# One-token attention over a 65,536-row cache with a gated FFN on one core: V partly past four columns of p, q in rows, wo in one bank, and looped programs

## The chip, the core and the metric

The kernel runs on one core of a Trainium2 chip. The metric is the device time of one execution in microseconds. Three runs of the kernel before gave 2518.55, 2518.58 and 2518.63 us (median 2518.58). The times inside the kernel come from one more execution, taken by the hardware profiler. Engines are called as the profile calls them: PE (matmul), PEld (its weight loads), DVE (vector), ACT (scalar), POOL, SP (which only issues transfers here).

## The reference, cut to what matters

```python
# B = Sq = 1, D = 512, H = 32 heads, Sk = 65536, Dh = 128, F = 1792, all bf16
q = (x @ wq).reshape(H, Dh)
scores = einsum("hd,hkd->hk", q, k_cache) * Dh ** -0.5
p = softmax(scores)
o = einsum("hk,hkd->hd", p, v_cache)
a = o.reshape(H * Dh) @ wo
b = (silu(x @ w_gate) * (x @ w_up)) @ w_down
g = sigmoid((x * gate_w).sum())
out = g * a + (1 - g) * b
```

K and V are 537 MB each and every byte of them is used once; the weights are about 14 MB.

## The kernel before

**Tiling.** A head's K and V come in two halves each ("first place" and "second place", u = 0 and 1). A half is 128 partitions of 256 rows of 128 numbers, 64 KB per partition and 8 MB in all, fetched by one transfer. The four places lie in one buffer `ring` of 176 KB per partition and overlap: K's second place begins in the middle of the first (32 KB against 0), V's first place at 96 KB and its second at 112 KB, `wq` at 144 KB for the start. So a transfer may be issued only when the part of the ring that it overwrites has been read.

**Order of the transfers.** SP issues them in one written-out list (L132-178): for head r, K's first place once half of the K second place before it is turned (`ktd`), V's second place of head r-1 once PE has passed rows 64 to 255 of V's first place (`va1`), K's second place once half of K's first is turned, V's first place once PE has finished the last head's V (`vbd`). Head 31 adds `wo`; then come the FFN weights, and the last head's V second place in six parts (`PARTS`, L114), whose last five wait for `va1`, so that PE can follow them as they land; the last two 128 KB slices of `w_down` end the list.

**Scores.** For each chunk of 16 rows DVE transposes 32-bit pairs into `kt` (`turn`, L274-278, four buffers), and PE runs four matmuls with `kt` moving, 512 columns each, against a sparse copy of q (`zq`), into `psS` (`scores`, L346-351). After both places DVE takes the maximum, POOL spreads it over the partitions, ACT takes the exponential into `pa`, DVE transposes it to `pb` (L300-302, L226-231).

**Values.** `values` (L353-358) runs one matmul per row of V: the 128x128 block of V is the stationary operand (it is loaded by a LDWEIGHTS), one column of `pb` moves past it, and the result gathers in one column of `psO`:

```python
last = nc.tensor.matmul(psO[:, 0:1], at(base + r * 256, Dh), pb[:, col:col + 1], ...)
```

**Order on PE.** A small loop of named bodies (L374-432): `pe_ka` (scores of K's first place), `pe_vb` (V's second place of the head before, waiting for the six marks `s_vb`, `s_p2` to `s_p6`, which for all heads but the last were counted up beforehand), `pe_kb` (scores of K's second place, then V's first place: rows 64 to 255, then 0 to 63). Before `pe_kb` of head 31 comes `pe_wo` (heads 0 to 30 times `wo`), after it `pe_mlp` (gate and up, 112 matmuls at L412, the wait for `guT`, then 12 slices of `w_down`), then `pe_vb` once more for head 31's V second place, and `pe_end` with the last slices and head 31's share of `wo`. Products with a row of `wo` or `w_down` go through `rows` (L360-364), as two matmuls of 256 columns, one into `psY` row 0 and one into `psZ` row 64.

**Other places that the change touches.** q is made by 128 matmuls with `wq` stationary and x moving (L335-339). SP, ACT and POOL have all 32 heads written out; DVE runs a loop over the heads; PE runs the bodies above.

Of the kernel before, what the change touches and what calls it, by code (L numbers as in the profile page):

```python
# [5 lines left out]
P = 128  # L6
KB = 1024
CH = 16
# [4 lines left out]
V_CUT = 64  # L13
# [13 lines left out]
def bass_gated_mix__mha_block_cached__swiglu_ffn__decode_kernel(  # L27
# [27 lines left out]
    with ExitStack() as ctx:  # L55
# [6 lines left out]
        def sem(name):  # L62
# [8 lines left out]
        psZ = psum("psZ", [P, 512], F32)  # L71

# [17 lines left out]
        fin = sb("fin", [P, D], BF16)  # L90
        sc = sb("sc", [P, 8], F32)
        xTb = sb("xTb", [P, 16], BF16)
# [5 lines left out]

        names = ("s_x s_wq s_k0a s_k0b s_ka s_kb s_va s_vb s_wo s_wo1 s_wg s_wu s_wd s_wd2 s_wd3 s_p2 s_p3 s_p4 s_p5 s_p6 "
                 "s_ones s_qd s_ramp s_rampT s_id s_sel s_z s_zb s_e1 s_g s_xT s_xTb s_q s_qTb s_qs s_zq s_h s_sig s_gu s_dch s_ach "  # L100
                 "ktd qkd va1 vbd s_mx s_ar s_nb s_exp s_pb s_L s_li s_otn s_o s_om s_wod s_o31 s_y0 s_y1 s_fin s_out")
# [12 lines left out]
        PARTS = ((192, 256), (0, 118), (118, 164), (164, 182), (182, 189), (189, 192))  # L114
# [17 lines left out]
        @block.sync  # L132
        def _(sp):
            def load(dst, src, s):
                sp.dma_start(dst, src).then_inc(sm[s], 16)  # L135

            def place(kind, h, u, s):
                byte = {"k": (K_A, K_B), "v": (V_A, V_B)}[kind][u]
                load(at(byte, ROWS * Dh), kv_dram[kind][h, u], s)

            k0 = kv_dram["k"][0, 0]
            k1 = kv_dram["k"][0, 1]
            half = ROWS * Dh // 2
            load(at(K_A + 2 * half, half), k0[:, half:2 * half], "s_ka")
            load(at(K_A, half), k0[:, 0:half], "s_k0a")
            load(at(K_B + 2 * half, half), k1[:, half:2 * half], "s_k0b")
            sp.wait_ge(sm["ktd"], NCH // 2)
            load(at(K_B, half), k1[:, 0:half], "s_kb")
            sp.wait_ge(sm["s_q"], 1)
            place("v", 0, 0, "s_va")  # L150
            for r in range(1, H):
                sp.wait_ge(sm["ktd"], PER * r - NCH // 2)
                place("k", r, 0, "s_ka")
                sp.wait_ge(sm["va1"], r)
                place("v", r - 1, 1, "s_vb")
                if r == L:
                    wo_dram = A_wo.rearrange("(p j) n -> p (j n)", j=32)
                    for q in range(2):
                        sp.wait_ge(sm["ktd"], PER * r + 3 * NCH // 4 + q * NCH // 4)
                        load(at(WO + q * 16 * KB, 16 * D), wo_dram[:, q * 16 * D:(q + 1) * 16 * D], "s_wo")  # L160
                sp.wait_ge(sm["ktd"], PER * r + NCH // 2)
                place("k", r, 1, "s_kb")
                sp.wait_ge(sm["vbd"], r + 1)
                place("v", r, 0, "s_va")
            sp.wait_ge(sm["s_wod"], 1)
            load(at(WG, Dc * F), B_w_gate.rearrange("(p c) f -> p (c f)", c=Dc), "s_wg")
            load(at(WU, Dc * F), B_w_up.rearrange("(p c) f -> p (c f)", c=Dc), "s_wu")
            load(at(WO1, D), A_wo[L * Dh:H * Dh, :], "s_wo1")
            sp.wait_ge(sm["ktd"], PER * H)
            wd_dram = B_w_down.rearrange("(p c) n -> p (c n)", c=FC)  # L170
            load(at(WD, WD_CUT * D), wd_dram[:, 0:WD_CUT * D], "s_wd")
            last = kv_dram["v"][L, 1]
            for n, ((r0, r1), s) in enumerate(zip(PARTS, MARKS)):
                if n == 1:
                    sp.wait_ge(sm["va1"], H)
                load(at(V_B + r0 * 256, (r1 - r0) * Dh), last[:, r0 * Dh:r1 * Dh], s)
            for j, s in ((FC - 2, "s_wd2"), (FC - 1, "s_wd3")):
                load(at(WD + 2 * j * D, D), wd_dram[:, j * D:(j + 1) * D], s)

        @block.gpsimd  # L180
        def _(pool):
            nc.gpsimd.memset(qd[:], 0.0).then_inc(sm["s_qd"], 1)
            for m, n in enumerate(MARKS[1:]):
                nc.gpsimd.memset(hbuf[:, m], 0.0).then_inc(sm[n], 16 * L)
            pool.wait_ge(sm["s_id"], 1)
            for je in range(4):
                off = 64 * (je // 2) + je % 2
                last = nc.gpsimd.tensor_copy(sel[:, je, :].rearrange("p (g d) -> p g d", g=4),  # L188
                                             ident[:, off:off + 63:2].unsqueeze(1).to_broadcast([P, 4, 32]))
            last.then_inc(sm["s_sel"], 1)  # L190
            for h in range(H):
                pool.wait_ge(sm["s_mx"], h + 1)
                nc.gpsimd.partition_all_reduce(amx, mxs, P, RMAX).then_inc(sm["s_ar"], 1)  # L193
                pool.wait_ge(sm["s_exp"], h + 2)
                pool.wait_ge(sm["s_li"], h + 1)  # L195
                nc.gpsimd.partition_all_reduce(Lt, rsum, P, RADD).then_inc(sm["s_L"], 1)  # L196

        @block.scalar
        def _(act):
# [12 lines left out]
            nc.scalar.activation(sc[:, 1:2], psW[:, 500:501], ACT.Exp, scale=-1.0).then_inc(sm["s_e1"], 1)  # L212
            act.wait_ge(sm["s_q"], 1)
            nc.scalar.copy(qTb[:], psM[:, 128:128 + H]).then_inc(sm["s_qTb"], 1)
            act.wait_ge(sm["s_qs"], 1)
            act.wait_ge(sm["s_qd"], 1)
# [4 lines left out]
            for h in range(H):  # L221
                if h == L:
                    act.wait_ge(sm["s_o"], 1)
                    nc.scalar.copy(om[:], psW[:, 0:32]).then_inc(sm["s_om"], 1)
                act.wait_ge(sm["s_ar"], h + 1)
                nc.scalar.mul(nbias, amx, -SCALE).then_inc(sm["s_nb"], 1)  # L226
                act.wait_ge(sm["s_nb"], h + 1)
                if h:
                    act.wait_ge(sm["s_pb"], h)
                nc.scalar.activation(pa[:], psS[:], ACT.Exp, bias=nbias, scale=SCALE,  # L230
                                     accum_out=rsum).then_inc(sm["s_exp"], 1)
                if h < L:
                    take_q(h + 1)
            act.wait_ge(sm["s_h"], 1)
            nc.scalar.activation(hbuf[:, 0, 0:FC], psM[:, 64:64 + FC], ACT.Exp, scale=-1.0).then_inc(sm["s_sig"], 1)  # L235
            act.wait_ge(sm["s_y1"], 1)
# [5 lines left out]
        def _(dve):  # L242
            chain = [0]

            def link(ins):
# [3 lines left out]

            nc.vector.memset(ones1[:], 1.0).then_inc(sm["s_ones"], 1)  # L250
# [11 lines left out]
                                    ALU.is_equal).then_inc(sm["s_id"], 1)  # L262
            dve.wait_ge(sm["s_x"], 32)
# [4 lines left out]
            nc.vector.tensor_copy(xTb[:, 0:Dc], psM[:, 0:Dc]).then_inc(sm["s_xTb"], 1)  # L268
# [11 lines left out]
            with nc.Fori(0, H, engines=[ET.DVE]) as i:  # L280
                dve.wait_ge(sm["s_ka"], i * 16 + 16)
                for n, c in enumerate(A_ORDER):
                    if n == NCH // 2:
                        dve.wait_ge(sm["s_k0a"], 16)
                    turn(K_A, c, n, i)
                    if n == 0:
                        dve.wait_ge(sm["s_otn"], i + 1)
                        dve.wait_ge(sm["s_L"], i + 1)
                        nc.vector.reciprocal(Li, Lt).then_inc(sm["s_li"], 1)
                dve.wait_ge(sm["vbd"], i + 1)  # L290
# [4 lines left out]
                for n, c in enumerate(B_ORDER):  # L295
                    if n == NCH // 2:
# [16 lines left out]
                                           in1=hbuf[:, 0, 0:FC], op0=ALU.mult, op1=ALU.mult).then_inc(sm["s_gu"], 1)  # L313
            dve.wait_ge(sm["vbd"], H + 1)
# [5 lines left out]
        def _(pe):  # L320
# [14 lines left out]
            for h in range(H):  # L335
                for c in range(Dc):
                    last = nc.tensor.matmul(psM[:, 128 + h:129 + h], wq_ap[:, c, h * Dh:(h + 1) * Dh],  # L337
                                            xTb[:, c:c + 1], start=(c == 0), stop=(c == Dc - 1))
# [20 lines left out]

            def rows(lhs, rhs, first=False, stop=False):  # L360
                half = D // 2
                a = nc.tensor.matmul(psY[0:1, 0:half], lhs, rhs[:, 0:half], start=first, stop=stop)  # L362
                b = nc.tensor.matmul(psZ[64:65, 0:half], lhs, rhs[:, half:D], start=first, stop=stop)  # L363
                return a, b

# [16 lines left out]
            with nc.body("pe_vb", valid_engines=only):  # L382
                i = nc.snap(head, min_val=1, max_val=H)
                for n, ((r0, r1), s) in enumerate(zip(PARTS, MARKS)):
                    pe.wait_ge(sm[s], i * 16)
                    last = values(V_B, 1, range(r0, r1), False, n == len(PARTS) - 1)
                last.then_inc(sm["vbd"], 1)
# [5 lines left out]
            with nc.body("pe_kb", valid_engines=only):  # L393
# [6 lines left out]
                values(V_A, 0, range(V_CUT, ROWS), True, False).then_inc(sm["va1"], 1)  # L400
                values(V_A, 0, range(0, V_CUT), False, False)
# [4 lines left out]
            with nc.body("pe_mlp", valid_engines=only):  # L406
# [8 lines left out]
                pe.wait_ge(sm["s_gu"], 1)  # L415
                pe.wait_ge(sm["s_wd"], 16)
                for j in range(WD_CUT):
                    rows(guT[:, j:j + 1], wd_ap[:, j, :])
                nc.br("pe_vb", engines=only)

            with nc.body("pe_wo", valid_engines=only):
# [7 lines left out]
                for j in range(32):  # L429
                    last = rows(om[:, j:j + 1], wo_ap[:, j, :], first=(j == 0))  # L430
                last[1].then_inc(sm["s_wod"], 1)
# [3 lines left out]
            pe.wait_ge(sm["s_wo1"], 16)  # L435
# [39 lines left out]
```

## Time and profile before

| what | us |
|---|---|
| median of three runs | 2518.58 |
| the profiled execution, its own time | 2518.55 |
| its span, first to last instruction | 2517.1 |
| PE busy / PEld / DVE | 1592.2 / 837.5 / 1221.9 |
| ACT busy / POOL | 40.3 / 25.4 |
| period of a head (exponential to exponential) | 77.4 |
| last byte of the ring's transfers landed | 2514.5 |

The profile's page gives each engine's busy time, 40 slices of the span, the transfer queues, the chain of work that ended last, and groups of instructions by line. The trace behind it answers further questions: the instructions in order of time (with the idle time before each and what ended it), who waited for whom, and busy time, granted TensorE clock and transfer rate for any stretch. In the order of time, runs of alike instructions are merged: "start, length, engine, line, operation, out<-in, xcount".

### The profile page before, as it was taken

The numbers are of one execution on the slowest core, as the hardware profiler recorded it, in microseconds if no ns is written. First come the engines' busy times: TensorE is split into PE (matmuls) and PEld (weight loads), VectorE is DVE, ScalarE is ACT, GpSimd is POOL, SyncE is SP. The second block draws the span as 40 slices with busy tenths as digits, with TensorE's granted clock in tenths as the row PEclk, the third lists the DMA queues.
The fourth block names the chain that finished last, engine by engine and source line by source line (L and its number), as shares of the span: only waits on it lengthen the run. The fifth ranks groups of instructions, "written<-read, shape, count | busy, mean of one in ns | idle before, by whom it ended". The sixth has DMA issues, their size and how long they took to land.

```text
span 2517.1 us, 45990 instructions
## 1 busy us (share of the span) xinstructions
PE 1592.2 (63%) x20829; PEld 837.5 (33%) x20829; DVE 1221.9 (49%) x1177; ACT 40.3 (2%) x138; POOL 25.4 (1%) x78
## 2 busy tenths in 40 slices
PE   4665765756657657666576575665765766657666
PEld 2333323323233233333332332323323333333234
DVE  4453553544535535445455354453553544545533
ACT  0000000000000000000000000000000000000000
POOL 0000000000000000000000000000000000000000
PEclk9776777767767767677677776776776767767776
DMA  9999999999999999999999999999999999999999
GB/s 418 434 435 433 435 433 434 433 434 434 433 433 433 433 433 433 433 433 433 433 433 433 432 433 433 433 433 433 433 434 433 433 433 433 433 433 433 434 431 401
DMA packets 20754, 1087.94 MB, mean 432 GB/s; under 512 B 2307, under 2 KB 2950, under 8 KB 3078
## 3 DMA queue, kind: packets, MB, share of 16 engines
q1 hardware_dynamic: 20736, 1087.78, 99.9%
q8 instruction: 8, 0.13, 0.0%
q14 instruction: 4, 0.03, 0.0%
q10 hardware_dynamic: 6, 0.00, 0.0%
HBM read 1087.77 MB, written 0.00 MB: 432 GB/s over the span
## 4 chain that ended last, share of the span: by engine, by line
issue 96%; ACT 1%; POOL 1%; DMA 1%; PE 0%; DVE 0%; SPq 0%; POOLq 0%
ACT pa L230 1%; DMA ring<-in_B_w_down_dram 1%; POOL st L196 0%; POOL st L193 0%; ACT st L226 0%; PE psO L356 0%; SPq L135 0%; POOL sel L188 0%; PE psY L362 0%; DVE pb L302 0%; POOLq L195 0%; DVE ramp L252 0%; DVE fin L317 0%; DVE zq L253 0%; DVE lt L254 0%
## 5 line engine op out<-in xcount | busy, mean ns | idle before, releaser
L349 PE MATMUL psS<-kt,zq 128*128 128x512 bf16 x4096 | 1133.8, 426 | 797.2 <-DVE kt L278 778.9
L278 DVE STREAM_TRANSPOSE kt<-ring 128x1024 uint32<-128x1024 uint32 x1024 | 1163.2, 1206 | 924.5 <-DMA ring<-in_A_k_cache_dram 924.5
L349 PEld LDWEIGHTS psS<-kt,zq 128*128 128x128 bf16 x4096 | 387.0, 104 | 1517.2 <-DVE kt L278 1054.6
L356 PE MATMUL psO<-pb,ring 128*128 128x1 bf16 x16384 | 439.1, 164 | 109.4 <-DVE pb L302 102.3
L356 PEld LDWEIGHTS psO<-pb,ring 128*128 128x128 bf16 x16384 | 433.6, 101 | 140.2 <-issue 122.0
L292 DVE TENSOR_SCALAR lt<-psO,st,sc 128x4 f32 x32 | 9.4, 294 | 246.8 <-PE psO L356 246.8
L302 DVE STREAM_TRANSPOSE pb<-pa 128x512 bf16<-128x512 bf16 x32 | 22.8, 712 | 48.7 <-ACT pa L230 48.7
L226 ACT ACTIVATE st<-st 128x1 f32<-128x1 f32 x32 | 6.5, 203 | 2383.8 <-POOL st L193 2383.8
L300 DVE TENSOR_REDUCE st<-psS 128x1 f32<-128x512 f32 x32 | 22.1, 691 | 37.5 <-PE psS L349 37.5
L193 POOL PARTITION_ALL_REDUCE st<-st x32 | 11.2, 350 | 2421.1 <-DVE st L300 2421.1
L230 ACT ACTIVATE pa<-psS,st 128x512 bf16<-128x512 f32 x32 | 22.0, 687 | 1.0
L196 POOL PARTITION_ALL_REDUCE st<-st x32 | 12.3, 383 | 36.4 <-ACT pa L230 36.4
L208 ACT COPY zq<-qd 128x16 bf16<-128x16 bf16 x32 | 7.9, 248 | 0.0
L362 PE MATMUL psY<-ring,om 128*1 128x256 bf16 x32 | 5.9, 372 | 2.4 <-DMA ring<-in_A_wo_dram 2.4
L315 DVE TENSOR_TENSOR o<-psO,st 128x1 bf16<-128x1 f32 x1 | 0.2, 161 | 14.5 <-PE psO L356 14.5
L309 DVE TENSOR_SCALAR hbuf<-hbuf 128x14 f32<-128x14 f32 x1 | 0.2, 175 | 13.9 <-ACT hbuf L235 13.9
L412 PE MATMUL psM<-xTb,ring 128*128 128x1 bf16 x112 | 6.9, 198 | 0.0
L412 PEld LDWEIGHTS psM<-xTb,ring 128*128 128x128 bf16 x112 | 6.8, 161 | 0.0
L230 ACT ACTIVATION_READ_ACCUMULATOR pa<-psS,st 128x1 f32 x32 | 6.2, 193 | 0.0
L337 PE MATMUL psM<-xTb,ring 128*128 128x1 bf16 x128 | 3.6, 165 | 3.9 <-DMA ring<-in_A_wq_dram 3.9
L363 PE MATMUL psZ<-ring,om 128*1 128x256 bf16 x32 | 5.9, 372 | 0.0
L362 PEld LDWEIGHTS psY<-ring,om 128*1 128x1 bf16 x32 | 3.6, 113 | 4.4 <-issue 2.5
(58 smaller groups left out, 35.7 us busy)
## 6 DMA issues: line engine op xcount, KB each, us to landing
ring<-in_A_k_cache_dram SPq DMA_DIRECT2D x4, 4096.0 KB, 27.3
ring<-in_A_wq_dram SPq DMA_DIRECT2D x1, 4096.0 KB, 12.2
ring<-in_A_wo_dram SPq DMA_DIRECT2D x2, 2048.0 KB, 10.6
ring<-in_A_v_cache_dram SPq DMA_DIRECT2D x1, 3776.0 KB, 18.0
ring<-in_A_v_cache_dram SPq DMA_DIRECT2D x1, 2048.0 KB, 18.2
ring<-in_B_w_gate_dram SPq DMA_DIRECT2D x1, 1792.0 KB, 36.9
ring<-in_B_w_up_dram SPq DMA_DIRECT2D x1, 1792.0 KB, 40.8
ring<-in_B_w_down_dram SPq DMA_DIRECT2D x1, 1536.0 KB, 13.7
```

Source lines behind the costliest of these rows:

```text
L193: nc.gpsimd.partition_all_reduce(amx, mxs, P, RMAX).then_inc(sm["s_ar"], 1)
L196: nc.gpsimd.partition_all_reduce(Lt, rsum, P, RADD).then_inc(sm["s_L"], 1)
L208: nc.scalar.copy(zq[:, :, 31:128:32], qd[:, h]).then_inc(sm["s_zq"], 1)
L230: nc.scalar.activation(pa[:], psS[:], ACT.Exp, bias=nbias, scale=SCALE, accum_out=rsum).then_inc(sm["s_exp"], 1)
L278: nc.vector.transpose(o, src).then_inc(sm["ktd"], 1)
L292: nc.vector.tensor_scalar(lt[:, bass.ds(i * 4, 4, P + 5)], psO[:, 0:1].to_broadcast([P, 4]), Li, sc[:, 3:4], ALU.mult, ALU.mult).then_inc( ...
L300: nc.vector.reduce_max(mxs, psS[:], AX_X).then_inc(sm["s_mx"], 1)
L302: nc.vector.transpose(pb[:], pa[:]).then_inc(sm["s_pb"], 1)
L349: last = nc.tensor.matmul(psS[:], zw[je][c], ktb[n % NB][:, je // 2, :, je % 2], start=first and je == 0, stop=stop and je == 3)
L356: last = nc.tensor.matmul(psO[:, 0:1], at(base + r * 256, Dh), pb[:, col:col + 1], start=first and n == 0, stop=stop and n == len(rows) - 1)
L362: a = nc.tensor.matmul(psY[0:1, 0:half], lhs, rhs[:, 0:half], start=first, stop=stop)
L412: last = nc.tensor.matmul(psM[:, o + j:o + j + 1], w[:, c, :, j], xTb[:, c:c + 1], start=(c == 0), stop=(c == Dc - 1))
```

## The change

- **Four columns of p.** A new function `flow` takes four rows of V in one matmul: four columns of `pb` are the stationary operand, and the four rows of V (512 numbers in each partition) move past them, into four rows of `psW`. Only the diagonal 128-column blocks of the result are wanted. V's second place: rows 192 to 255 and 0 to 55 go this way (120 rows, 30 matmuls); V's first place: rows 64 to 155 and 0 to 63 (156 rows, 39 matmuls). `values` keeps the other 136 and 100 rows. Per head DVE copies the four rows of `psW` to `brow`, and PE adds the four diagonal blocks to `psO` by four small f32 matmuls after the third part.
- **q in rows.** x, in column 0 of blocks of 32 otherwise zero columns (`xTz`), is stationary and `wq` moves past it, 32 matmuls of 512 columns in four column strips; ACT copies the two banks, and eight matmuls turn the rows to columns.
- **wo in one bank.** `whole` does a row of `wo`, and 12 slices of `w_down`, as one matmul of 512 columns into a new bank `psF`; ACT copies that row to `brow`, and a pair of f32 matmuls starts `psY` and `psZ` with it.
- **Loops.** SP runs heads 1 to 30 and ACT heads 0 to 30 in a loop with computed addresses and waits. Two waits go (POOL's for `s_li`, ACT's for `s_pb`); the wait for `s_wo1` moves forward.
- The second part of the last V grows from 118 to 120 rows.

```diff
-        PARTS = ((192, 256), (0, 118), (118, 164), (164, 182), (182, 189), (189, 192))
+        PARTS = ((192, 256), (0, 120), (120, 164), (164, 182), (182, 189), (189, 192))
+        FLOW = 2
+        B_FLOW = 56
+        A_FLOW = 156
...
-            for r in range(1, H):
-                sp.wait_ge(sm["ktd"], PER * r - NCH // 2)
-                place("k", r, 0, "s_ka")
...
+            with nc.Fori(0, L - 1, engines=[ET.SP]) as i:
+                head(i, False)
+            head(L - 1, True)
...
+            with nc.Fori(0, L, engines=[ET.Activation]) as i:
+                softmax(i)
+                nc.scalar.copy(zq[:, :, 31:128:32],
+                               qd[:, bass.ds(i + 1, 1)].rearrange("p a e g -> p (a e) g")).then_inc(sm["s_zq"], 1)
...
+            act.wait_ge(sm["s_y"], 1)
+            nc.scalar.copy(brow[0:1, :], psF[0:1, :]).then_inc(sm["s_br"], 1)
...
+                dve.wait_ge(sm["s_fl"], i + 1)
+                nc.vector.tensor_copy(brow[0:4, :], psW[0:4, :]).then_inc(sm["s_flc"], 1)
                 dve.wait_ge(sm["vbd"], i + 1)
...
-            for h in range(H):
+            for b, bank in enumerate((psY, psZ)):
                 for c in range(Dc):
-                    last = nc.tensor.matmul(psM[:, 128 + h:129 + h], wq_ap[:, c, h * Dh:(h + 1) * Dh],
-                                            xTb[:, c:c + 1], start=(c == 0), stop=(c == Dc - 1))
+                    for k in range(4):
+                        n0 = (4 * b + k) * D
+                        last = nc.tensor.matmul(bank[32 * k:32 * k + 32, :], xTz[:, 32 * c:32 * c + 32],
+                                                wq_ap[:, c, n0:n0 + D], start=(c == 0), stop=(c == Dc - 1))
...
+            def flow(base, u, rows, first, stop):
+                for n, r in enumerate(rows[::4]):
+                    col = (r % CH) * 32 + NCH * u + r // CH
+                    last = nc.tensor.matmul(psW[0:4, :], pb[:, col:col + 97:32], at(base + r * 256, 4 * Dh),
+                                            start=first and n == 0, stop=stop and n == len(rows) // 4 - 1)
+                return last
...
+            def whole(lhs, rhs, first=False, stop=False):
+                return nc.tensor.matmul(psF[0:1, :], lhs, rhs, start=first, stop=stop)
...
                     pe.wait_ge(sm[s], i * 16)
+                    if n == 0:
+                        flow(V_B, 1, range(r0, r1), False, False)
+                        continue
+                    if n == 1:
+                        flow(V_B, 1, range(r0, B_FLOW), False, True).then_inc(sm["s_fl"], 1)
+                        r0 = B_FLOW
                     last = values(V_B, 1, range(r0, r1), False, n == len(PARTS) - 1)
+                    if n == FLOW:
+                        pe.wait_ge(sm["s_flc"], i + 1)
+                        for e in range(4):
+                            nc.tensor.matmul(psO[:, 0:1], brow[0:4, e * Dh:(e + 1) * Dh], id4[0:4, e:e + 1],
+                                             start=False, stop=False)
...
-                values(V_A, 0, range(V_CUT, ROWS), True, False).then_inc(sm["va1"], 1)
-                values(V_A, 0, range(0, V_CUT), False, False)
+                flow(V_A, 0, range(V_CUT, A_FLOW), True, False)
+                values(V_A, 0, range(A_FLOW, ROWS), True, False).then_inc(sm["va1"], 1)
+                flow(V_A, 0, range(0, V_CUT), False, False)
...
                 for j in range(WD_CUT):
-                    rows(guT[:, j:j + 1], wd_ap[:, j, :])
+                    last = whole(guT[:, j:j + 1], wd_ap[:, j, :], stop=(j == WD_CUT - 1))
+                last.then_inc(sm["s_y"], 1)
+                pe.wait_ge(sm["s_br"], 1)
+                rows(onesr[0:1, 0:1], brow[0:1, :], first=True)
...
-                    last = rows(om[:, j:j + 1], wo_ap[:, j, :], first=(j == 0))
-                last[1].then_inc(sm["s_wod"], 1)
+                    last = whole(om[:, j:j + 1], wo_ap[:, j, :], first=(j == 0))
+                last.then_inc(sm["s_wod"], 1)
```

More of the change, by code (lines that the diff above doesn't have):

```diff
@@ L71, in bass_gated_mix__mha_block_cached__swiglu_ffn__decode_kernel @@
         psZ = psum("psZ", [P, 512], F32)
+        psF = psum("psF", [P, 512], F32)
         ring = sb("ring", [P, RING // 2], BF16)
@@ L90, in bass_gated_mix__mha_block_cached__swiglu_ffn__decode_kernel @@
         fin = sb("fin", [P, D], BF16)
+        brow = sb("brow", [P, D], F32)
+        id4 = sb("id4", [P, 4], F32)
         sc = sb("sc", [P, 8], F32)
-        xTb = sb("xTb", [P, 16], BF16)
+        xTz = sb("xTz", [P, 4 * 32], BF16)
         qTb = sb("qTb", [P, H], BF16)
@@ L97, in bass_gated_mix__mha_block_cached__swiglu_ffn__decode_kernel @@
         mxs, amx, nbias, rsum, Lt, Li = (st[:, i:i + 1] for i in range(6))
+        qrow = brow[:].bitcast(BF16)
+        xTb = xTz[:, 0:97:32]
         names = ("s_x s_wq s_k0a s_k0b s_ka s_kb s_va s_vb s_wo s_wo1 s_wg s_wu s_wd s_wd2 s_wd3 s_p2 s_p3 s_p4 s_p5 s_p6 "
                  "s_ones s_qd s_ramp s_rampT s_id s_sel s_z s_zb s_e1 s_g s_xT s_xTb s_q s_qTb s_qs s_zq s_h s_sig s_gu s_dch s_ach "
-                 "ktd qkd va1 vbd s_mx s_ar s_nb s_exp s_pb s_L s_li s_otn s_o s_om s_wod s_o31 s_y0 s_y1 s_fin s_out")
+                 "ktd qkd va1 vbd s_mx s_ar s_nb s_exp s_pb s_L s_li s_otn s_o s_om s_y s_br s_fl s_flc s_id4 s_qr s_qc s_wod s_o31 s_y0 s_y1 s_fin s_out")
         sm = {n: sem(n) for n in names.split()}
@@ L138, in place @@
                 byte = {"k": (K_A, K_B), "v": (V_A, V_B)}[kind][u]
-                load(at(byte, ROWS * Dh), kv_dram[kind][h, u], s)
+                src = kv_dram[kind][:, u]
+                if isinstance(h, int):
+                    src = src[h]
+                else:
+                    src = src[bass.ds(h, 1)].rearrange("h p n -> (h p) n")
+                load(at(byte, ROWS * Dh), src, s)
             k0 = kv_dram["k"][0, 0]
@@ L150, in _, with head @@
             place("v", 0, 0, "s_va")
-            for r in range(1, H):
-                sp.wait_ge(sm["ktd"], PER * r - NCH // 2)
-                place("k", r, 0, "s_ka")
-                sp.wait_ge(sm["va1"], r)
-                place("v", r - 1, 1, "s_vb")
-                if r == L:
+            def head(r, late):
+                sp.wait_ge(sm["ktd"], r * PER + (PER - NCH // 2))
+                place("k", r + 1, 0, "s_ka")
+                sp.wait_ge(sm["va1"], r + 1)
+                place("v", r, 1, "s_vb")
+                if late:
                     wo_dram = A_wo.rearrange("(p j) n -> p (j n)", j=32)
                     for q in range(2):
-                        sp.wait_ge(sm["ktd"], PER * r + 3 * NCH // 4 + q * NCH // 4)
+                        sp.wait_ge(sm["ktd"], r * PER + (PER + 3 * NCH // 4 + q * NCH // 4))
                         load(at(WO + q * 16 * KB, 16 * D), wo_dram[:, q * 16 * D:(q + 1) * 16 * D], "s_wo")
[L161 to L164, printed above, removed]
+                sp.wait_ge(sm["ktd"], r * PER + (PER + NCH // 2))
+                place("k", r + 1, 1, "s_kb")
+                sp.wait_ge(sm["vbd"], r + 2)
+                place("v", r + 1, 0, "s_va")
+            with nc.Fori(0, L - 1, engines=[ET.SP]) as i:
+                head(i, False)
+            head(L - 1, True)
             sp.wait_ge(sm["s_wod"], 1)
@@ L181, in _ @@
         def _(pool):
+            nc.gpsimd.memset(xTz[:], 0.0).then_inc(sm["s_qd"], 1)
             nc.gpsimd.memset(qd[:], 0.0).then_inc(sm["s_qd"], 1)
@@ L194, in _ @@
                 pool.wait_ge(sm["s_exp"], h + 2)
-                pool.wait_ge(sm["s_li"], h + 1)
                 nc.gpsimd.partition_all_reduce(Lt, rsum, P, RADD).then_inc(sm["s_L"], 1)
@@ L212, in _ @@
             nc.scalar.activation(sc[:, 1:2], psW[:, 500:501], ACT.Exp, scale=-1.0).then_inc(sm["s_e1"], 1)
+            for b, bank in enumerate((psY, psZ)):
+                act.wait_ge(sm["s_qr"], b + 1)
+                nc.scalar.copy(qrow[:, b * D:(b + 1) * D], bank[:]).then_inc(sm["s_qc"], 1)
             act.wait_ge(sm["s_q"], 1)
@@ L215, in _ @@
             act.wait_ge(sm["s_qs"], 1)
-            act.wait_ge(sm["s_qd"], 1)
+            act.wait_ge(sm["s_qd"], 2)
             for g in range(4):
@@ L220, in _, with softmax @@
             take_q(0)
-            for h in range(H):
-                if h == L:
-                    act.wait_ge(sm["s_o"], 1)
-                    nc.scalar.copy(om[:], psW[:, 0:32]).then_inc(sm["s_om"], 1)
+            def softmax(h):
                 act.wait_ge(sm["s_ar"], h + 1)
@@ L227, in _ @@
                 act.wait_ge(sm["s_nb"], h + 1)
-                if h:
-                    act.wait_ge(sm["s_pb"], h)
                 nc.scalar.activation(pa[:], psS[:], ACT.Exp, bias=nbias, scale=SCALE,
                                      accum_out=rsum).then_inc(sm["s_exp"], 1)
-                if h < L:
-                    take_q(h + 1)
+            with nc.Fori(0, L, engines=[ET.Activation]) as i:
+                softmax(i)
+                nc.scalar.copy(zq[:, :, 31:128:32],
+                               qd[:, bass.ds(i + 1, 1)].rearrange("p a e g -> p (a e) g")).then_inc(sm["s_zq"], 1)
+            act.wait_ge(sm["s_o"], 1)
+            nc.scalar.copy(om[:], psW[:, 0:32]).then_inc(sm["s_om"], 1)
+            softmax(L)
             act.wait_ge(sm["s_h"], 1)
             nc.scalar.activation(hbuf[:, 0, 0:FC], psM[:, 64:64 + FC], ACT.Exp, scale=-1.0).then_inc(sm["s_sig"], 1)
+            act.wait_ge(sm["s_y"], 1)
+            nc.scalar.copy(brow[0:1, :], psF[0:1, :]).then_inc(sm["s_br"], 1)
             act.wait_ge(sm["s_y1"], 1)
@@ L248, in link @@
                 dve.wait_ge(sm["s_dch"], chain[0])
+            nc.vector.memset(psW[:], 0.0).then_inc(sm["s_fl"], 1)
             nc.vector.memset(ones1[:], 1.0).then_inc(sm["s_ones"], 1)
@@ L262, in _ @@
                                     ALU.is_equal).then_inc(sm["s_id"], 1)
+            dve.wait_ge(sm["s_id"], 1)
+            nc.vector.tensor_copy(id4[:], ident[:, 0:4]).then_inc(sm["s_id4"], 1)
             dve.wait_ge(sm["s_x"], 32)
@@ L267, in _ @@
             dve.wait_ge(sm["s_xT"], 1)
-            nc.vector.tensor_copy(xTb[:, 0:Dc], psM[:, 0:Dc]).then_inc(sm["s_xTb"], 1)
+            dve.wait_ge(sm["s_qd"], 2)
+            nc.vector.tensor_copy(xTb, psM[:, 0:Dc]).then_inc(sm["s_xTb"], 1)
             dve.wait_ge(sm["s_e1"], 1)
@@ L313, in _ @@
                                            in1=hbuf[:, 0, 0:FC], op0=ALU.mult, op1=ALU.mult).then_inc(sm["s_gu"], 1)
+            dve.wait_ge(sm["s_fl"], H + 1)
+            nc.vector.tensor_copy(brow[0:4, :], psW[0:4, :]).then_inc(sm["s_flc"], 1)
             dve.wait_ge(sm["vbd"], H + 1)
@@ L334, in _ @@
             pe.wait_ge(sm["s_wq"], 16)
-            for h in range(H):
+            for b, bank in enumerate((psY, psZ)):
                 for c in range(Dc):
-                    last = nc.tensor.matmul(psM[:, 128 + h:129 + h], wq_ap[:, c, h * Dh:(h + 1) * Dh],
-                                            xTb[:, c:c + 1], start=(c == 0), stop=(c == Dc - 1))
+                    for k in range(4):
+                        n0 = (4 * b + k) * D
+                        last = nc.tensor.matmul(bank[32 * k:32 * k + 32, :], xTz[:, 32 * c:32 * c + 32],
+                                                wq_ap[:, c, n0:n0 + D], start=(c == 0), stop=(c == Dc - 1))
+                last.then_inc(sm["s_qr"], 1)
+            pe.wait_ge(sm["s_id"], 1)
+            for b in range(2):
+                pe.wait_ge(sm["s_qc"], b + 1)
+                if b == 0:
+                    pe.wait_ge(sm["s_id4"], 1)
+                for j in range(4):
+                    h = 128 + 16 * b + j
+                    last = nc.tensor.matmul(psM[:, h:h + 13:4], qrow[:, b * D + j * Dh:b * D + (j + 1) * Dh],
+                                            ident[:, 0:97:32], start=True, stop=True)
             last.then_inc(sm["s_q"], 1)
@@ L415, in _ @@
                 pe.wait_ge(sm["s_gu"], 1)
+                pe.wait_ge(sm["s_wo1"], 16)
                 pe.wait_ge(sm["s_wd"], 16)
                 for j in range(WD_CUT):
-                    rows(guT[:, j:j + 1], wd_ap[:, j, :])
+                    last = whole(guT[:, j:j + 1], wd_ap[:, j, :], stop=(j == WD_CUT - 1))
+                last.then_inc(sm["s_y"], 1)
+                pe.wait_ge(sm["s_br"], 1)
+                rows(onesr[0:1, 0:1], brow[0:1, :], first=True)
                 nc.br("pe_vb", engines=only)
@@ L429, in _ @@
                 for j in range(32):
-                    last = rows(om[:, j:j + 1], wo_ap[:, j, :], first=(j == 0))
-                last[1].then_inc(sm["s_wod"], 1)
+                    last = whole(om[:, j:j + 1], wo_ap[:, j, :], first=(j == 0))
+                last.then_inc(sm["s_wod"], 1)
                 nc.br("pe_kb", engines=only)
             nc.switch_bb("pe_end")
-            pe.wait_ge(sm["s_wo1"], 16)
             pe.wait_ge(sm["s_wd2"], 16)
```

## The prediction

> **What bounds the kernel now.** I read the page's slices and queues first, then the timeline of the last 50 us, then one head in the middle, then the granted clock by stretches.
>
> ```profile
> DMA  9999999999999999999999999999999999999999
> ...
> q1 hardware_dynamic: 20736, 1087.78, 99.9%
> q8 instruction: 8, 0.13, 0.0%
> q14 instruction: 4, 0.03, 0.0%
> ```
>
> The transfers fill the span: 1087.8 MB at the 433 GB/s of the middle slices take 2510 us of 2517.1. In the chain of waits 96% is "issue", so that view names no bound; the queue does. A head costs 77.4 us because 33.55 MB take that long, and no saved PE, ACT or POOL time can shorten it. What can move is the start (about 2 us), the tail, and the middle if a transfer is issued too late. First the middle, in order of time:
>
> ```profile
> 1319.56 0.33 SPq L135 DMA_DIRECT2D ring<-in_A_v_cache_dram  x1
> 1330.54 1.25 DVE L278 STREAM_TRANSPOSE kt<-ring 128x1024 uint32<-128x1024 uint32 x1 [16.48 <-DMA ring<-in_A_k_cache_dram]
> ...
> 1356.65 0.33 SPq L135 DMA_DIRECT2D ring<-in_A_v_cache_dram  x1
> ...
> 1369.23 18.14 DVE L278 STREAM_TRANSPOSE kt<-ring 128x1024 uint32<-128x1024 uint32 x16 [12.17 <-DMA ring<-in_A_k_cache_dram]
> ```
>
> Each V transfer is issued 11.0 and 12.6 us before the K transfer ahead of it has landed (DVE starts then). That is the cover of PE's V work. Now the tail:
>
> ```profile
> 2485.14 6.95 PE L356 MATMUL psO<-pb,ring 128*128 128x1 bf16 x256 [3.19 <-DVE pb L302]
> ...
> 2491.95 6.86 PE L412 MATMUL psM<-xTb,ring 128*128 128x1 bf16 x112
> ...
> 2500.12 0.37 PE L362 MATMUL psY<-ring,guT 128*1 128x256 bf16 x1 [1.30 <-DVE guT L312]
> ...
> 2502.77 1.86 PE L356 MATMUL psO<-pb,ring 128*128 128x1 bf16 x64
> ...
> 2508.46 3.30 PE L356 MATMUL psO<-pb,ring 128*128 128x1 bf16 x118 [3.82 <-DMA ring<-in_A_v_cache_dram]
> ...
> 2512.00 2.50 PE L356 MATMUL psO<-pb,ring 128*128 128x1 bf16 x74 [0.24 <-DMA ring<-in_A_v_cache_dram]
> ```
>
> From 2485.1 PE works almost without pause; its only slack is 3.8 us before 2508.46 and 0.2 us after. From the end of the values (2514.5) to the end of the span it is 2.6 us. So whatever is added to PE here beyond 4 us moves the end.
>
> **The prices.** A values matmul costs 27 ns (256 in 6.95 us; 25 at full clock). For 512 columns the price hangs on the granted clock:
>
> ```profile
> 2379.80:2396.90 17.10, 14.55 (x58) 4.67 (x56) 14.52 (x14) 0.91 (x4) 0.35 (x1) 1.00 0.99 429
> 2396.90:2405.10 8.20, 6.98 (x256) 6.90 (x256) 0.71 (x1) 0.22 (x2) 0.38 (x1) 0.50 0.98 424
> 2415.40:2420.80 5.40, 5.31 (x13) 1.89 (x14) 5.40 (x7) 0.00 (x0) 0.00 (x0) 0.50 1.15 498
> ...
> 2443.30:2448.10 4.80, 4.76 (x46) 3.02 (x48) 0.00 (x0) 0.00 (x0) 0.00 (x0) 0.50 1.02 437
> 2448.10:2451.50 3.40, 1.19 (x22) 0.74 (x18) 0.00 (x0) 0.00 (x0) 0.00 (x0) 1.00 0.89 386
> ```
>
> After stretch and length come PE, PEld, DVE, ACT and POOL, then the clock. From start to start of L349 I get 427 ns per 512 columns at 0.50, and 225 at 1.00. The clock changes every 3.41 us or multiples: over the whole trace it rose after windows that streamed 77% or more of the time and not after 75% or less; it fell after 36% or less and not after 37%. One-column values do not hold it (second line: PE busy, 0.50). One-column `rows` of 256 do lift it (last two lines), so I take it that `flow` and `whole` do too. [...]
>
> **The change, part by part.** *Middle.* V's first place up to `va1`: 23 streams for 92 values, 23 x 0.225 - 92 x 0.027 = +2.7 us (+7.3 at half clock). V's second place: 30 streams for 120 values, plus four f32 matmuls: +4.6 us (+10.6). Cover 11.0 and 12.6 us: nothing, in both cases. If the cover went, each us late would cost 31 us. DVE's copy of `psW` (L300, as large, 0.69 us) stands ahead of L292, which waits for PE 8 us anyway; what is behind it, the transposes, waits for K. No row shows an SP transfer with a computed address; a written one takes 0.33 us, DVE's computed waits show no gap, and 6 us are free at each V, so I take nothing. The ACT loop and the two dropped waits lie beside 75 us of idle.
>
> *Start.* q: 8 groups of four strips, 8 x 0.43 = 3.4 us if the strips run together as the pairs of `rows` do, 13.7 if not, then a copy (L230: 0.69) and eight small matmuls, for 3.6 us before: +1 to +12 us. zq is ready at 19.4, scores start at 25.2, and the transfers issued have work until about 40 while SP is next needed at 33.1: nothing at either end.
>
> *wo.* 32 `whole` at 11 x 0.427 + 21 x 0.225 = 9.4 us for 5.9. Next on PE is K at 2462.7 and the FFN weights stand 30 us deep in the queue: nothing.
>
> *Programs.* Instruction packets are 0.16 MB, 0.4 us of the queue at most: -0.4 to 0, taken as 0 because the tail ends on PE.
>
> *Tail, from 2485.14.* (a) 23 streams: half clock until about 2489.0, 9 x 0.427 + 14 x 0.225 = 7.0. (b) 100 values 2.7, so `va1` at 2494.8, 4 us later; SP's last seven transfers wait for it, but the queue still holds the 2 MB part issued at 2481.2, landing 18.2 us later at 2499.4: hidden. (c) 16 streams 3.6. (d) L412 6.8 at the clock of that row (0.50), since one-column matmuls let it fall. (e) ACT and DVE to `guT` 1.3. (f) 12 `whole` at 0.427, the clock being down: 5.1 (12 pairs took 2.6). (g) ACT's copy of 512: between L237 (256, 0.36) and L230 (0.69), 0.55, with two semaphores 0.75. (h) f32 `rows`: L331 in f32 took 0.58 where L323 took 0.16 in bf16, so 0.21 to 0.85 for 256 columns; 0.85. Sum: 2513.2, against 2502.6 before. The 120-row part has then landed (2508.6), so the slack is gone. (i) 16 + 14 streams, the clock lifted by (f): 6.8. (j) 64 + 44 values 2.9. (k) four f32 matmuls at 0.15 (bf16, as L323) to 0.58 (L331): 0.25 each, being pipelined, 1.0. (l) 28 values 0.75. (m) the end 2.6. That is 2527.3. The profiled execution took 1.45 us more than its span and lies 0.03 us under the median: **2528.7 us**, +0.40%. Where the clock's windows fall shifts this by 1.2 us either way, (g), (h), (k) by -1 to +1.5.
>
> **Rivals.**
> 1. *L412 follows the clock.* Its 60 ns show at 0.50 alone; as cycles they would be 30 ns at 1.00, and (c) leaves the clock up for a window or so. -3.5: 2525 (2522.5 to 2527). For: values stay at 25 to 27 ns at either clock only because they are at another limit. Against: L412's strided weights may be bound by reading.
> 2. *The clock stays at 1.00 throughout the tail, and the end is not slower.* All the streams together hold it up: (a) 5.2, (b) 2.5, (c) 3.6, (d) 3.4, (e) 1.3, (f) 2.7, (g) and (h) 1.2: 2505.0; (i) 16 streams to 2508.6, just as the part lands, 14 more, then 1.6, 1.1, 1.0, 0.7 and 2.6: 2518.8, with 1.45 2520.3, +0.07%. It decides if PE comes to V before about 2508. Against: L412 holds PE 3.4 us or more with one-column work, over which the clock fell each time above.
> 3. *The streams do not lift the clock.* All at 0.427: (a) to (h) end at 2519.4, the end is 2540, so 2541, and more if V's issue starves. Against: the `rows` line.
> 4. *PE is not what ends the tail, and shorter programs gain*: the last byte sets the end, 0.4 us less: 2518.2, no measurable change; over 0.2% faster only if unseen fetches slow the queue now. The trace records 12 such packets in 2517 us, while PE jumps between its bodies about 130 times. [...]
> 5. *Streams run closer together than any row shows.* [...] The 4096 matmuls of L349 are never closer than 0.22.
>
> **How the numbers follow.** The sum 0.57, rival 1 0.23, rival 2 0.10, rival 3 0.05, rival 4 0.02 over 0.2% faster, rival 5 0.03. The range leaves out rivals 2 to 5 (0.20) and takes in the sum's bounds and rival 1's: 2522 to 2533. A run can tell 0.2% (5.04 us, 2523.6) from no change. Slower: the sum, rival 3 and nearly all of rival 1, 0.83; faster 0.02; the rest, 0.15, within.
>
> **What would show it.** Right: the period of a head stays 77.4; in the last 35 us PE never waits for a transfer of V, `whole` steps by about 0.43 us, the streams for part one start near 2513, and the last byte lands at 2514 to 2515 as before, 10 us ahead of the last values. Wrong: a wait of PE for V's second part (rival 2), L412 under 6 us (rival 1), clock 0.50 through the streams (rival 3), or a DMA slice below 9 in the middle, which would void the cover.

## The result and the profile after

The changed kernel takes 2528.47 us (median of six runs, 2527.43 to 2530.16); beside them the kernel before took 2518.55 us. The ratio is 1.004, with an interval of 1.003 to 1.0049: slower by 9.9 us. The profiled execution is the longest of the six, 2530.16 us with a span of 2528.7.

First the page of the kernel after: the granted clock in 40 slices, and the queues.

```profile
PEclk9888888878888878888788888888888888988887
DMA  9999999999999999999999999999999999999997
...
q1 hardware_dynamic: 20736, 1087.78, 99.5%
q8 instruction: 5, 0.08, 0.0%
q14 instruction: 2, 0.02, 0.0%
```

The queue is as full as before up to the last slice alone, where it falls to 7. Instruction packets fell from 12 to 7. The granted clock rose from 0.725 to 0.844 on the whole, as the streams hold it up (0.727 in the kernel without them, 0.907 in the one with all rows streamed, both below), but no time was won by it. Now the middle of the kernel after, in order of time (start, length):

```profile
1323.79 0.33 SPq L143 DMA_DIRECT2D ring<-in_A_v_cache_dram  x1
1330.46 1.25 DVE L307 STREAM_TRANSPOSE kt<-ring 128x1024 uint32<-128x1024 uint32 x1 [16.48 <-DMA ring<-in_A_k_cache_dram]
...
1361.82 0.33 SPq L143 DMA_DIRECT2D ring<-in_A_v_cache_dram  x1
...
1369.15 18.14 DVE L307 STREAM_TRANSPOSE kt<-ring 128x1024 uint32<-128x1024 uint32 x16 [6.91 <-DMA ring<-in_A_k_cache_dram]
```

The two V transfers are now issued 6.7 and 7.3 us ahead of the landing of K, where it was 11.0 and 12.6. The period of a head is still 77.40 us, head 31's exponential ends at 2484.0 (before: 2484.1), and the last byte of the ring's transfers lands at 2514.35 (before: 2514.46). So up to there the two kernels are level. The rest is the tail, as the chain of waits has it (start, length, engine, tile, line):

```profile
2485.12 6.81 PE psW L408 x23
2491.94 2.58 PE psO L401 x100
2494.52 5.24 PE psW L408 x16
2499.76 6.83 PE psM L479 x112
...
2507.87 5.12 PE psF L419 x12
2513.02 0.58 ACT brow L260
...
2514.24 6.57 PE psW L408 x30
2520.81 2.82 PE psO L401 x108
2523.63 1.79 PE psO L451 x8
2525.42 0.84 PE psO L401 x28
```

PE never waits for a transfer in it. When the last byte lands at 2514.35, PE has just begun the 30 streams of V's second place; it ends the values at 2526.26, 11.8 us later than before (2514.50).

### The profile page after: what moved, and what is told of

It reads as the page before. It is cut to its first block, busy times and chain, and to the rows that moved or that the text cites. A ratio compares the mean times of both kernels' runs of the same rounds, so it can differ in the third digit from the quotient of the medians.

```text
span 2528.7 us, 33495 instructions
## 1 busy us (share of the span) xinstructions
PE 1965.4 (78%) x14333; PEld 833.9 (33%) x14333; DVE 1244.7 (49%) x1212; ACT 42.0 (2%) x141; POOL 25.5 (1%) x79
## 4 chain that ended last, share of the span: by engine, by line
DMA 73%; DVE 15%; issue 8%; PE 2%; DVEq 1%; SPq 0%; ACT 0%; POOL 0%
DMA ring<-in_A_k_cache_dram 73%; DVE kt L307 15%; PE psS L394 1%; PE psW L408 1%; DVEq L304 0%; PE psM L479 0%; PE psO L401 0%; PE psF L419 0%; SPq L143 0%; DVE st L318 0%; PE psO L451 0%; PE psY L414 0%; ACT pa L247 0%; DVE pb L333 0%; DVE st L331 0%
## 5 line engine op out<-in xcount | busy, mean ns | idle before, releaser
L408 PE MATMUL psW<-ring,pb 128*4 128x512 bf16 x2208 | 570.1, 421 | 102.3 <-DVE pb L333 102.3
L408 PEld LDWEIGHTS psW<-ring,pb 128*4 128x4 bf16 x2208 | 200.4, 94 | 455.0 <-issue 231.4
L401 PEld LDWEIGHTS psO<-pb,ring 128*128 128x128 bf16 x7552 | 196.4, 96 | 28.3 <-issue 27.8
L401 PE MATMUL psO<-pb,ring 128*128 128x1 bf16 x7552 | 204.6, 164 | 0.0
L320 DVE COPY brow<-psW 4x512 f32<-4x512 f32 x32 | 21.7, 678 | 240.2 <-PE psW L408 240.2
L451 PE MATMUL psO<-id,brow 4*128 4x1 f32 x256 | 42.4, 283 | 0.0
L451 PEld LDWEIGHTS psO<-id,brow 4*128 4x128 f32 x256 | 39.7, 233 | 0.6
L419 PE MATMUL psF<-ring,om 128*1 128x512 bf16 x32 | 9.8, 481 | 0.3 <-ACT om L255 0.3
L252 ACT COPY zq<-qd 128x16 bf16 x31 | 7.7, 248 | 0.0
L346 DVE COPY brow<-psW 4x512 f32<-4x512 f32 x1 | 0.7, 678 | 13.0 <-PE psW L408 13.0
L479 PEld LDWEIGHTS psM<-xTz,ring 128*128 128x128 bf16 x112 | 6.8, 162 | 0.4 <-issue 0.4
```

Of the source, the lines that this page charges most:

```text
L320: nc.vector.tensor_copy(brow[0:4, :], psW[0:4, :]).then_inc(sm["s_flc"], 1)
L408: last = nc.tensor.matmul(psW[0:4, :], pb[:, col:col + 97:32], at(base + r * 256, 4 * Dh), start=first and n == 0, stop=stop and n == len( ...
L419: return nc.tensor.matmul(psF[0:1, :], lhs, rhs, start=first, stop=stop)
L451: nc.tensor.matmul(psO[:, 0:1], brow[0:4, e * Dh:(e + 1) * Dh], id4[0:4, e:e + 1], start=False, stop=False)
```

## The experiments

My theory: all of the loss is PE's work between the last softmax and the end, less 3.8 us of slack. The rivals: the middle loses something in every head; `whole` is the larger part; shorter programs gain something. Each kernel ran beside the kernel before on the same chip.

**No streams.** `flow` undone, `whole`, q in rows and loops kept.

```diff
-                flow(V_A, 0, range(V_CUT, A_FLOW), True, False)
-                values(V_A, 0, range(A_FLOW, ROWS), True, False).then_inc(sm["va1"], 1)
-                flow(V_A, 0, range(0, V_CUT), False, False)
+                values(V_A, 0, range(V_CUT, ROWS), True, False).then_inc(sm["va1"], 1)
+                values(V_A, 0, range(0, V_CUT), False, False)
...
+                    last = values(V_B, 1, range(r0, r1), False, n == len(PARTS) - 1)
```

> The changed kernel with every row of V back in one-column values matmuls; whole, q in rows and the loops stay. My theory (PE's work in the tail after the last softmax is all of the loss, and there are 3.8 us of slack): the streams and the four f32 matmuls go, and whole with its copy adds 4 us ahead of V's second part, which the slack takes: PE comes to part one near 2506 and to part two near 2508.6 as it lands, 2518.5 us (2518.2 to 2519.0). Rival (whole is the larger part of the loss, or the pieces add up without slack): 2522 or more.

Measured: 2518.65 us (before: 2518.65). Ratio 1.000 (0.9991 to 1.0009). In order of time in this kernel:

```profile
2505.79 1.81 PE L397 MATMUL psO<-pb,ring 128*128 128x1 bf16 x64
2508.91 5.88 PE L397 MATMUL psO<-pb,ring 128*128 128x1 bf16 x192 [1.31 <-DMA ring<-in_A_v_cache_dram]
```

PE comes to part one 3 us later than before (2502.77), because of `whole`, and still waits 1.31 us for part two. `whole` alone costs nothing: the slack takes it.

**No `whole`.** `rows` in the place of `whole` for `wo` and `w_down`, the copy and the f32 pair gone, streams kept.

```diff
-                    last = whole(guT[:, j:j + 1], wd_ap[:, j, :], stop=(j == WD_CUT - 1))
-                last.then_inc(sm["s_y"], 1)
-                pe.wait_ge(sm["s_br"], 1)
-                rows(onesr[0:1, 0:1], brow[0:1, :], first=True)
+                    rows(guT[:, j:j + 1], wd_ap[:, j, :])
```

> The changed kernel with wo and w_down back in pairs of 256 columns; the streams of V stay. My theory: the chain is shorter by 3.7 us ahead of V's second place (5.1 to 2.6 for the twelve rows, copy and f32 pair gone), of which up to 1.5 us are lost again because the shorter rows lift the clock less often before the 30 streams: 2525.8 us (2524.5 to 2527). Rival (whole explains most of the loss): under 2522.

Measured: 2525.07 us (before: 2518.65), ratio 1.0027 (1.0017 to 1.0038). So `whole` costs some 3.5 us once the streams have used up the slack, and none without them; the streams cost 6.4 us alone. What a stream costs follows the granted clock (in the changed kernel 216 ns from start to start at 1.00, 427 at 0.50), and so depends on where the clock changes, which in that trace is always on a grid of 3.41 us. In the kernel without `whole` the first 23 took 5.1 us, the price at 1.00, against 6.8 in the changed kernel, where the clock fell to 0.50 at 2485.4:

```profile
2485.26 5.12 PE L406 MATMUL psW<-ring,pb 128*4 128x512 bf16 x23 [3.23 <-DVE pb L331]
```

**Both undone.** q in rows, the loops and the parts of 120 and 44 rows remain.

> Both undone: what is left of the change is q in rows, the loops of SP and ACT, the shorter programs and the two rows moved between the last V's parts. My theory: nothing, 2518.1 to 2518.7 us, with fewer instruction packets than before. Rival (shorter programs free the transfer queue): 2518.1 or less by 0.4 us or more; rival (computed transfers or the later q cost): over 2519.

Measured: 2518.56 us (before: 2518.65), ratio 1.000 (0.9991 to 1.0009), with 9 instruction packets for 12. Shorter programs gained nothing that can be measured, and q in rows and the loops cost nothing.

**The last head by values.** Streams in heads 0 to 30, the last head in bodies of its own (`pe_va_last`, `pe_vb_last`) with `values` for all rows, and `rows` for `whole`.

```diff
+                nc.br_lt(left, 3, on_true="pe_va_last", on_false="pe_va", engines=only)
...
+            with nc.body("pe_va_last", valid_engines=only):
+                values(V_A, 0, range(V_CUT, ROWS), True, False).then_inc(sm["va1"], 1)
+                values(V_A, 0, range(0, V_CUT), False, False)
+                nc.br("pe_mlp", engines=only)
```

> The streams stay in heads 0 to 30 (30 and 39 a head), the last head alone goes through one-column values in bodies of its own, and wo in pairs. My theory: V's transfers keep 4 us and more of their cover in the middle, so the streams cost nothing there: 2518.5 us (2518.1 to 2519), period 77.4. Rival (part of the 10 us is lost in the middle, a third of a microsecond in every head): 2521 to 2528.

Measured: 2524.88 us (before: 2518.65), ratio 1.0025 (1.0015 to 1.0034). My number failed, but not for the rival's reason: the period is 77.40 and head 31's exponential ends at 2484.5, 0.4 us later than before. The other 6 us come after it. In order of time, the lines at which PE stood idle (in brackets: how long, and for what):

```profile
2491.85 3.57 PE L397 MATMUL psO<-pb,ring 128*128 128x1 bf16 x128 [4.45 <-issue]
2497.78 2.27 PE L397 MATMUL psO<-pb,ring 128*128 128x1 bf16 x79 [2.35 <-issue]
2517.26 2.51 PE L397 MATMUL psO<-pb,ring 128*128 128x1 bf16 x88 [2.12 <-issue]
```

With 1.29 us at the end that is 10.2 us of waiting for nothing but issue, most of it in the middle of runs of alike matmuls; and its page has 14 packets of 16 KB on q8, ten of them after 2448 us. My bodies had made PE's program longer by about 1000 instructions. That gave a new theory, that code entered late must be fetched, which the run "Never-run code" below tests.

**All rows streamed in the middle.** The same with all 512 rows of heads 0 to 30 through `flow`.

> As the kernel with values in the last head, but heads 0 to 30 put all 512 rows of V through the four-column streams: 128 streams a head, 27.6 us at full clock. The cover read from the kernel before is 11.0 us at V's second place and 12.6 at its first. My theory: va1 comes 5.6 to 8 us later than before, vbd about 10 us later (streams, then DVE's copy and the f32 matmuls in the open), still in time: 2518.5 us (to 2520), period 77.4. Rival (the cover is less than read, as a transfer needs some us from its issue to its first byte): 1 us or more a head, over 2549.

Measured: 2556.06 us (before: 2518.54), ratio 1.0147 (1.0131 to 1.0162). This theory fell, and the rival's number held. In order of time in this kernel:

```profile
1309.78 0.33 SPq L143 DMA_DIRECT2D ring<-in_A_v_cache_dram  x1
...
1313.39 18.14 DVE L305 STREAM_TRANSPOSE kt<-ring 128x1024 uint32<-128x1024 uint32 x16 [3.20 <-DMA ring<-in_A_k_cache_dram]
```

The V transfer is issued 3.6 us ahead of K's landing (4.6 at the other place), and yet the period rose from 77.40 to 78.66 us and the last exponential came 39 us later. Being ahead is not enough. How much is needed can be read from the marks with which the transfers report that they have landed, for all V transfers between 100 and 2400 us. In the kernel before, each landed 19.34 to 19.36 us after the K transfer ahead of it. In this kernel the 11 that were issued 4.85 us or more ahead of that landing kept this distance (19.31 to 19.38 us); of the 47 that were issued closer to it, 36 landed more than 0.1 us later than that, at most 21.3 us after it. So some 4.9 us are enough, and less often is not.

**Four strips.** The matmuls of `flow` go in turn to result rows 0, 32, 64 and 96 of `psW`, so to four column strips of the array; rows 0 to 63 of part two and 64 to 159 of V's first place go through it; `brow` takes all rows, and `id4` sums over the strips.

```diff
-                    last = nc.tensor.matmul(psW[0:4, :], pb[:, col:col + 97:32], at(base + r * 256, 4 * Dh),
-                                            start=first and n == 0, stop=stop and n == len(rows) // 4 - 1)
+                    k = 32 * (n % 4)
+                    last = nc.tensor.matmul(psW[k:k + 4, :], pb[:, col:col + 97:32], at(base + r * 256, 4 * Dh),
+                                            start=first and n < 4, stop=stop and n >= len(rows) // 4 - 4)
```

> The changed kernel with the streams of V spread over four column strips of the array (result rows 0, 32, 64, 96 of psW), 64 rows of the last part and 160 of the first stream, whole kept. The 16 matmuls of q in rows ran four at a time (16 in 1.7 to 1.9 us at 512 columns each). My theory: four rows then cost 54 ns at full and 107 at half clock, against 216 and 427: the streams cost no more than values, whole's 4 us fall into the slack, what is left is the four f32 matmuls late in the tail: 2519.5 us (2518.3 to 2520). Rival (strips of 4 columns do not run together): 2528 as before.

Measured: 2519.75 us (before: 2518.54), ratio 1.0005 (0.9996 to 1.0014).

```profile
2485.29 2.73 PE L412 MATMUL psW<-ring,pb 128*4 128x512 bf16 x24 [3.19 <-DVE pb L336]
...
2490.46 1.04 PE L412 MATMUL psW<-ring,pb 128*4 128x512 bf16 x16
...
2513.37 1.84 PE L455 MATMUL psO<-id,brow 128*128 128x1 f32 x8
```

24 streams in 2.73 us, where 23 in one strip took 6.81. With that the whole loss but 1.2 us is gone, which shows again that it was the length of the streams in the tail. The expectation put the 1.2 us down to the f32 matmuls; the last run tests that.

**Strips without `whole`.**

> The same with wo and w_down in pairs of 256 columns. My theory: the slack was already enough, so no further gain: 2519.5 us (2518.3 to 2520), the rest being the f32 matmuls behind the landing of the third part. Rival (whole's 4 us still show): 2 to 4 us less than the kernel with whole and strips.

Measured: 2519.78 us (before: 2518.54): no further gain, as the slack had been enough.

**Never-run code.** The kernel before, with 400 matmuls in a body that no branch enters.

```diff
-                nc.br_lt(head, H, on_true="pe_ka", on_false="pe_mlp", engines=only)
+                nc.br_lt(head, H, on_true="pe_ka", on_false="pe_gate", engines=only)
+            with nc.body("pe_gate", valid_engines=only):
+                nc.br_lt(head, 1, on_true="pe_pad", on_false="pe_mlp", engines=only)
+            with nc.body("pe_pad", valid_engines=only):
+                values(V_A, 0, range(0, ROWS), False, False)
+                values(V_A, 0, range(0, 144), False, False)
+                nc.br("pe_mlp", engines=only)
```

> [...] The streams-but-last kernel lost 6.3 us though its heads kept 77.40 us: PE stood idle 4.5, 2.4, 2.1 and 1.3 us in the tail on nothing but issue, and 10 instruction packets of 16 KB came after 2448 us, where the changed kernel has one. Theory (PE's program no longer fits what the engine keeps, so bodies entered late must be fetched behind a full transfer queue): more instruction packets late, idle on issue at jumps of the tail, 2522 to 2530 us. Rival (its loss came from its other branches or from the streams): 2518.6 as before, no more packets.

Measured: 2529.88 us (before: 2518.57), ratio 1.0044 (1.003 to 1.0058), with 18 packets on q8 for 8.

```profile
2492.33 3.56 PE L356 MATMUL psO<-pb,ring 128*128 128x1 bf16 x128 [2.62 <-issue]
2498.81 0.70 PE L356 MATMUL psO<-pb,ring 128*128 128x1 bf16 x21 [2.93 <-issue]
2505.74 5.47 PE L420 MATMUL psM<-xTb,ring 128*128 128x1 bf16 x89 [6.23 <-issue]
```

The work is that of the kernel before, and PE idles on issue for 15.4 us in the tail. The records of the packets fit: in this kernel and in the one with the last head by values, each of the nine idles of over 1.2 us that the profile puts down to issue, among the values and the matmuls of gate and up and at the end, follows a packet on q8 and ends 1.3 to 1.7 us after it has landed. The idle of 1.75 us ahead of 2521.77 lies wholly after the last byte of the other transfers (2516.0), so a full queue is not needed for such an idle. So code that is not run can cost 11 us. The kernel with the last head by values has the same signs, and its 10.2 us of idle less some 4 us of slack are its 6.2 us.

**Strips, and the f32 matmuls early.** The strip kernel without `whole`, in which V's second place streams part one alone, and the copy and the f32 matmuls stand ahead of the wait for part two.

```diff
                     if n == 0:
-                        flow(V_B, 1, range(r0, r1), False, False)
-                        continue
-                    if n == 1:
-                        flow(V_B, 1, range(r0, B_FLOW), False, True).then_inc(sm["s_fl"], 1)
...
+                        flow(V_B, 1, range(r0, r1), False, True).then_inc(sm["s_fl"], 1)
+                        pe.wait_ge(sm["s_flc"], i + 1)
...
+                        continue
```

> The four-strip kernel with pairs of 256 columns, but V's second place streams its first part alone (64 rows), and DVE's copy and the four f32 matmuls come right behind it, ahead of the wait for the second part; the second part is values again. In the strip kernels PE ran without pause from 2508.7 to 2515.9 us, 1.7 us of it the f32 matmuls. My theory: these then lie in the slack ahead of 2508.6, the last 1.2 us go, 2518.5 us (2518.2 to 2518.8). Rival (something else in the strips costs the 1.2 us, the middle or the last byte): 2519.7 as the other strip kernels.

Measured: 2518.71 us (before: 2518.57), ratio 1.000 (0.9991 to 1.0009).

```profile
2506.04 1.05 PE L447 MATMUL psO<-id,brow 128*128 128x1 f32 x8 [0.81 <-DVE brow L347]
2509.19 5.87 PE L402 MATMUL psO<-pb,ring 128*128 128x1 bf16 x192 [2.10 <-DMA ring<-in_A_v_cache_dram]
```

PE waits 2.10 us for part two again, and the 1.2 us are gone. No version beats the kernel before: in the three that are as fast as it (no streams, both undone, this one) and in the kernel before itself the last byte lands between 2514.5 and 2515.0, and the span ends 2.5 to 2.6 us behind it.

## Why the prediction was right

The bound, the place and the cause were as forecast: nothing changes until the last softmax, and the tail adds up on PE. Step by step, forecast against the chain of the kernel after (us):

| step | forecast | measured |
|---|---|---|
| (a) 23 streams | 7.0 | 6.82 |
| (b) 100 values | 2.7 | 2.58 |
| (c) 16 streams | 3.6 | 5.24 |
| (d) 112 matmuls of gate and up | 6.8 | 6.83 |
| (e) to `guT` | 1.3 | 1.28 |
| (f) 12 `whole` | 5.1 | 5.12 |
| (g) copy, (h) f32 pair | 1.6 | 1.25 |
| (i) 30 streams | 6.8 | 6.57 |
| (j) 108 values | 2.9 | 2.82 |
| (k) four f32 matmuls | 1.0 | 1.79 |
| (l) 28 values | 0.75 | 0.84 |
| (m) the end | 2.6 | 2.44 |

The steps measured are 1.45 us longer in sum than those forecast: (c) and (k) were 2.4 us too short, and the others together 1.0 us too long. These are the steps of the longest of the six runs; that the forecast lies only 0.2 us from their median, 2528.47, is luck, as the runs differ by 2.7 us. **(c)**: I let the clock stay up over (b), though one-column values did not hold it. The stretches of the kernel after (start and end, length, PE, PEld, DVE, ACT, POOL, clock) show it:

```profile
2488.80:2495.60 6.80, 6.80 (x121) 4.16 (x120) 0.00 (x0) 0.00 (x0) 0.00 (x0) 1.00 1.02 428
2495.60:2499.00 3.40, 3.40 (x10) 1.07 (x9) 0.00 (x0) 0.00 (x0) 0.00 (x0) 0.50 1.13 481
...
2499.70:2502.40 2.70, 2.70 (x46) 2.70 (x46) 0.00 (x0) 0.00 (x0) 0.00 (x0) 1.00 1.06 455
2502.40:2506.60 4.20, 4.17 (x70) 4.09 (x69) 0.00 (x0) 0.00 (x0) 0.00 (x0) 0.51 0.90 387
```

(b) ran from 2491.9 to 2494.5 at 1.00, and the stretch from 2495.6 to 2499.0 was granted 0.50. **(k)**: an f32 matmul ran as two, 214 ns apart at 0.50 and 112 at 1.00, so four cost 1.8 or 0.9 us; I had 0.25 each. Where the changes of the clock fall probably also spreads the six runs over 2.7 us, where those of the kernel before lie within 0.24; with one trace of the changed kernel this is not shown.

**Rival 1 fell.** The last two lines are the matmuls of (d): 46 in 2.70 us at 1.00 and 70 in 4.2 at 0.51, 60 ns at either clock. **Rivals 2 and 3 fell** with the clock column: it goes up and down through the tail, and the streams do lift it: from 2485.4 to 2488.8 they ran alone on PE at 0.50, and from 2488.8 the clock was 1.00. **Rival 4 fell** with the kernel that keeps only loops and q. Its other half, that fetching instructions costs time, shows in neither of the two kernels (one packet each on q8 after 2440 us, and no idle on issue behind it), but the run with never-run code shows that it can. With the never-run code the packets of 16 KB on q8 rose from 8 to 18. That PE's program had outgrown what the engine keeps is my explanation; no run measures what it keeps. A fetch at every jump is not what the traces show, as in the kernel before no packet came on q8 between 163 and 2443 us, while PE jumped between its bodies in some 29 heads. **Rival 5 fell**: streams in one strip stood 216 ns apart at full clock and 427 at half.

**The middle** was forecast at no cost, and had none, but with less to spare than the text said: it counted 11.0 and 12.6 us of cover as usable to the end, while the kernel with all rows streamed shows that some 4.9 us of it are needed. The head shown above had 6.7 and 7.3, but of the changed kernel's 59 V transfers between 100 and 2400 us five were issued only 5.3 to 5.6 us ahead. All still landed at the old distance (19.33 to 19.37 us), with some 0.4 us to spare.

## What to carry to other kernels

Price each piece of a changed tail against the slack ahead of the next landing: here two pieces of about 4 and 10 us of PE work, ahead of which lay 4 us of slack, cost 0 and 6.4 alone and 9.9 together. A matmul with one or four stationary columns and 512 moving ones cost almost what one with 128 did here (216 ns from start to start at a granted clock of 1.00, against 225); sent to four column strips in turn, 24 of those with four took 2.73 us. Before adding code for a special case, look how many instruction packets come late in the run (here one, against eleven with the never-run code): "issue" ahead of a long run of alike matmuls was the sign (idles of up to 6.2 us).

## What the runs showed of the hardware

- 400 matmuls in a body that never runs cost 11.3 us: in the tail PE idled on issue for 0.2 to 6.2 us at a time, 15.4 us in all, and each of the five idles of over 1.2 us follows a packet of 16 KB.
- Four streams of 512 columns in four column strips ran together: 24 in 2.73 us, against 6.81 for 23 in one strip.
- With all rows streamed, V transfers issued 4.85 us or more ahead of the landing of the one before them lost nothing; 36 of the 47 issued 2.9 to 4.8 us ahead came late, by up to 1.9 us, and a head took 1.26 us longer.
- 112 matmuls with weights read at a stride of 28 bytes took 60 ns each at granted clocks of 0.5 and 1.0, where values took 27 and 25.
